# Feature columns in another order, sums over slots first, and another instruction list, in a fused attention and feed-forward kernel

## The chip, the cores and the metric

The kernel runs on one core of a Trainium2 chip. The metric is device time in microseconds (us) of one execution; before the change the median of three runs is 409.5 us (409.31 to 409.65). The engines are named as the profile names them: PE is TensorE (matmuls), PEld its weight loads, DVE is VectorE, ACT is ScalarE, POOL is GpSimd, SP is SyncE, which here issues nearly all transfers.

## What is computed

One transformer block on x of 2048 rows and 576 columns, in bf16. A vector c gives six modulation vectors (`silu(c) @ w_mod`): shift, scale and gate for each of two halves.

```
h = layernorm(x) * (1 + ca) + sa
x = x + ga * A(h)            # attention with feature maps, 32 heads of 18
h = layernorm(x) * (1 + cb) + sb
x = x + gb * (relu(h @ w1) @ w2)      # 576 -> 4608 -> 576
```

The attention has no score matrix. Queries and keys go through a map of 18 x 18 per head, and each gives 36 features:

```
q, k, v = split(h @ wqkv)                       # heads of 18
pq, pk = q @ w_phi[h], k @ w_phi[h]
phi = concat([softmax(p), softmax(-p)], -1)     # over the 18 features of a head
kv = phi_k^T v;  z = sum over rows of phi_k
o = (phi_q @ kv) / (phi_q @ z + 1e-6);  A = o @ wo
```

## The kernel before, in words

The 2048 rows are 16 tiles of 128 (four blocks of four tiles; eight units of two tiles). The work has three stages.

In the first, up to about 18 us, the weights are prepared. The key map is folded into the key weights: SP loads `kv_raw` (five chunks of the weights of keys and values, step `LK`) and the first blocks of x (`LP`); TensorE transposes each chunk (`fold_T`, step `WT`, line 341), DVE or ACT copies it out (`WTE`), TensorE multiplies by the maps (`fold`, `F1`, line 351), and DVE or ACT copies the result out in two pieces (`FA1`, `FB1`). Beside it run the layer norms of the first tiles (`LS` statistics, `RS` the reciprocal root, `LX` the normalization; the statistics of units 1, 4, 6 and 7 are on ACT, lines 230 and 231) and the modulation columns (`first_mods`, `MC1`, line 319, copied out at lines 324 to 328). `Z` is a dummy matmul (line 205).

In the second stage, 18 to 88 us, each tile's values, keys and queries are projected (`proj`, line 457; steps `V`, `K`, `Q`) into PSUM tiles of two banks, of which there are three (`mmp`), and copied out by ACT or DVE (`VE`, `KE`, `QE`, all at lines 88 and 90). The keys' features go through the softmaxes block by block. Then the products of features and values over all 16 tiles are summed (`kv_part`, `KVa` to `KVc`, line 636).

In the third, the eight units of queries are taken through their softmax, a transposing transfer (`q_T`, step `qT`, line 664, tile ET), the product with kv (`num`, line 677), the quotient, the product with wo, the second layer norm and the feed-forward (`ps_h` at line 807, ReLU at lines 863, 864 and 890, `ps_y` at line 907).

A tile's features stand in 11 groups of three heads. A group has 54 numbers per sign: 18 features by 3 heads, with the head innermost. Two features side by side make a slot of 6 numbers (pair, head), so there are 9 slots. The softmax of both signs is made by `softmax_parts`, for the keys on four tiles at a time (line 606), for the queries on two (line 616). The steps are, with the names in the order list (with a `q` in front for queries):

- `MN`, `MX` (`ext`): minimum and maximum over the features, a tree of operations on DVE (lines 474 to 479).
- `LO`, `HI` (`less`): minimum minus feature and feature minus maximum, written to the two halves of the group (lines 487 and 489), both into bf16.
- `EX`: exp on ACT, in place (line 516).
- `SU`, then `SA`: sums over the slots by TensorE, nine matmuls with the identity into PSUM (line 523), and over the pairs by DVE (line 527). Seven pairs of key tiles and one unit of queries go this way. All others take `SD` (`sums`, line 534): one reduction on DVE over all 18 features.
- `RC`: ln and exp on ACT, which make the reciprocal (lines 539 and 541); `SC`: scaling on DVE, one operation for keys (line 547) and one per sign for queries (line 551).

Within a group the layout is sign, slot, pair, head: 54 numbers of the one sign, then 54 of the other.

Instructions of SP, PE, DVE and ACT run in the order in which the code gives them. For the first 145 us or so that is the list of steps `order` in the kernel's text: a step is a name with its place (tile, chunk or unit), and a last number, where there is one more, says which of DVE and ACT takes a copy. After the list the blocks of the remaining units follow in loops (`block`), with fixed places for the softmax steps of the next units. A list item that stands earlier is ahead in the queue of each engine that it uses, transfers on SP included.

Of the kernel before, what the change touches and what calls it, by code (L numbers as in the profile page):

```python
# [43 lines left out]
def kernel(  # L44
# [419 lines left out]
    def softmax_parts(E, src, n, whole):  # L464
# [3 lines left out]
        def slots(a, s=0):  # L468
            return a[:, :, :, s * GF:(s + 1) * GF].rearrange("p n g (f c) -> p (n g) f c", c=G2)

        def ext(op):
            src_, w = src.rearrange("p n g c -> p (n g) c"), 4 * G2
            a = work.tile([P, 4 * NG, w], BF16, name="tree", tag="tree", bufs=1)[:, 0:ng]
            V.tensor_tensor(out=a, in0=src_[:, :, 0:w], in1=src_[:, :, w:2 * w], op=op)
            for w in (2 * G2, G2):
                V.tensor_tensor(out=a[:, :, 0:w], in0=a[:, :, 0:w], in1=a[:, :, w:2 * w], op=op)  # L476
            V.tensor_tensor(out=a[:, :, 0:G2], in0=a[:, :, 0:G2], in1=src_[:, :, 8 * G2:9 * G2], op=op)
# [40 lines left out]
        def sums_pe(j):  # L518

            ps = t["s", j] = aux_tile("ps_sum")[:, 0:2 * NG * 2 * G2].rearrange("p (a c) -> p a c", c=G2)  # L520
            e = E[:, j:j + 2].rearrange("p n g (s c) -> p (n g) s c", s=2)
            for f in range(DH // 2):
                T_.matmul(ps, lhsT=ident[:], rhs=e[:, :, :, f * G2:(f + 1) * G2], start=(f == 0), stop=(f == DH // 2 - 1))  # L523
# [6 lines left out]
        def sums(j):  # L530
            b, k = j // 2 * 2, j % 2
            if ("l", b) not in t:
                t["l", b] = work.tile([P, 4 * NG, GH], FP32, name="ln_s", tag="ln_s", bufs=2)
            V.tensor_reduce(out=t["l", b][:, k * 22:(k + 1) * 22].rearrange("p (g s) h -> p g s h", s=2), op=ALU.add,  # L534
                            axis=mybir.AxisListType.X, in_=E[:, j].rearrange("p g (s f h) -> p g s h f", s=2, h=GH))
# [7 lines left out]
        def scale(j):  # L543
            r = t["r", j][:].rearrange("p a e h -> p a (e h)")
            if whole:
                e = E[:, j:j + 2].rearrange("p n g (s f c) -> p (n g s) f c", s=2, c=G2)
                V.tensor_tensor(out=e, in0=e, in1=r.unsqueeze(2).to_broadcast([P, 4 * NG, DH // 2, G2]), op=ALU.mult)
                return
            for s in range(2):
                e, q = slots(E[:, j:j + 2], s), r.rearrange("p (a s) c -> p a s c", s=2)[:, :, s]  # L550
                V.tensor_tensor(out=e, in0=e, in1=q.unsqueeze(2).to_broadcast([P, 2 * NG, DH // 2, G2]), op=ALU.mult)
# [13 lines left out]
    def pad_keys(b):  # L565
        G.memset(phik_g(b)[:, :, NG - 1, 0:GF], 0.0)
# [17 lines left out]
    def features(dst, ps, eng):  # L584

        copy(eng, dst[:, 0:10, :].rearrange("p (a g) c -> p a g c", a=2),
             ps[:, :, 0:5 * GF].rearrange("p a (g c) -> p a g c", c=GF))
        copy(eng, dst[:, 10, :].rearrange("p (f h) -> p f h", h=GH)[:, :, 0:2],
             ps[:, 1, 5 * GF:5 * GF + 36].rearrange("p (f h) -> p f h", h=2))

    def keys_out(t, eng):
        features(phik_g(t // TPB)[:, t % TPB, :, 0:GF], pss["k", t], eng)

    def queries_out(t, eng):
# [4 lines left out]
        features(pq[b][:, j], pss["q", t], eng)  # L599
# [5 lines left out]
    def k_soft(b):  # L605
        return softmax_parts(phik_g(b), phik_g(b)[:, :, :, 0:GF], TPB, True)
# [3 lines left out]
    def q_soft(n):  # L610
# [5 lines left out]
        return softmax_parts(E[:, :, :, 0:DW], pq[b][:, u * U:(u + 1) * U], U, False)  # L616
# [356 lines left out]
    LH LK.0 Z.21 LP.1 SIL CR LP.0 Z.22 Z.11 LK.4 Z.3 WT.0 LS.3 LS.1 LK.1 LS.2 WT.4 Z.8 WBD WTE.4 WT.1 WTE.1.1 WTE.0  # L973
    LK.2 RS.1 Z.20 WT.2 LK.3 LS.0 LA F1.1 LX.1 RS.0 WTE.2.1 WT.3 FA1.1 FB1.1 WTE.3.1 LX.0 LP4.2 Z.23 F1.2 F1.4 FB1.4.1
    FB1.2.1 Z.24 FA1.4.1 PT.1 MC1.0 PX.1.0 PX.1.1 PT.0 PX.0.0.1 FA1.2 F1.0 FA1.0 PX.0.1 F1.3 MC1.1 MC1.2 FA1.3.1
    FB1.0.1 MSC MSH SCv.2 FB1.3.1 SCv.0 LP4.4 SCv.3 Bv SCv.4 LP4.6 SCv.1.1 BEv.0.1 LQ.1 B1 LS.6 OPEN BE1.1.1 LQ.5
    BEv.1.1 SC1.0 SC1.3 PM.0 LS.5 V.3 BE1.0.1 V.1 LQ.4 SC1.4.1 V.0 LQ.3 VE.3 LS.4 SC1.2 LS.8 SC1.1 VE.1 PM.2 VE.0 RS.2
    LQ.2 LS.7 LQ.0 LX.2 LS.12 V.2 K.0 K.1 LT.5 RS.3 VE.2.1 KE.0.1 LT.4 LS.9 KE.1.1 K.2 KE.2 F0.0 LS.11 K.3 FB0.0.1
    FA0.0.1 F0.4 LS.13 LX.3 PM.1 FA0.4 FB0.4 V.5 LS.10 KE.3 VE.5 RS.4 SC0.0 V.4 LT.7 VE.4 F0.2 FB0.2.1 FA0.2.1 MN.0
    LO.0 SC0.4.1 K.5 LT.6 F0.1 K.7 LX.4 KE.5 K.6 FA0.1.1 FB0.1 LO.1 F0.3 SC0.2 LM.2 MX.0 LT.8 SC0.1 KE.7 FA0.3.1 K.4  # L980
    FB0.3.1 KE.6 SC0.3 KE.4 MN.1 RS.5 B0 BE0.1.1 V.7 LX.5 LM.0 BE0.0.1 LS.14 LM.1 HI.1 PM.3 Q.2 LT.10 VE.7 QE.2 RS.6
    Q.1 HI.0 K.8 QE.1 LT.11 Q.7 KE.8.1 MX.1 EX.0 QE.7 LS.15 Q.0 LX.6 Q.3 LO.3 QE.0 RS.7 SU.0 K.10 LT.9 QE.3.1 HI.3 K.11
    K.9 EX.1 KE.11 LO.2 WOL qMN.0 SA.0 LX.7 KE.10 KE.9 LT.12 SU.1 HI.2 EX.3 K.12 RW.1 RW.0 MN.2 SA.1 qMX.0 KE.12 LT.15
    SU.3 RWE.0.1 LT.14 K.15 RC.0 W1 qLO.0 K.14 RWE.1.1 LO.4 EX.2 KE.15 qHI.0 LT.13 Q.14 LO.5 MX.2 SA.3 KE.14 qEX.0
    QE.14 K.13 V.9 RC.1 HI.5 SU.2 HI.4 RC2.0 KE.13 MN.3 Q.4 LW.1.1 LO.7 VE.9 qEX.1 SA.2 V.8 EX.4 EX.5 QE.4.1 Q.13 MX.3
    V.6 VE.8 LO.6 SC.0 qSU.0 V.13 RC.2 SC.2 VE.6 qSA.0 RD.2 QE.13 Q.12 SU.5 RC.3 HI.6 VE.13 SC.3 qRC.0 V.10 EX.6 SU.4
    VE.10 SA.5 RC2.2 V.11 RC.5 QE.12 VE.11 qSC.0 V.12 SA.4 HI.7 EX.7 SC.1 SD.12 Q.8 V.15 RD.0 SD.13 SC.5 VE.12 VE.15
    SU.7 RC.4 SA.7 SC.4 RC.6 V.14 qT.0 QE.8 KVa LW.1.0 SC.6 VE.14 RC.7 KVb RC2.1 SC.7 LW.0.0 KVc Q.11 WS.1 KVE.0 LW.2.1
    KVE.1 LW.0.1 QE.11 WS.0 NU.1 Q.6 NU.0 NUE.1 OT.1 Q.10 NUE.0 qMN.1 OT.0 OTE.1 QE.6 OTE.0 MCE2 WO.1 QE.10 WOE.1 WO.0
    WOE.0 S2.1.1 R2.1 S2.0 R2.0 Q.15 X2.1 X2.0 Q.9 qLO.1 PN.1 PN.0 QE.15 PNE Q.5 QE.5 QE.9 qMX.1 qHI.1 qEX.3 HA.0 HA.1  # L990
    HA.2 qMN.2 HB.0 LW.2.0 P2 HB.1 qSD.3 qEX.2 HB.2 qSD.2 LW.3.1 qMX.2 LW.3.0 W2.0.0 W2.1.0 RL.0 W2.0.1 HA.3 RL.1 qRC.1
    RL.2 RD.1 HA.4 HB.3 HB.4 HA.5 RL.3 HA.6 W2.2.1 HB.5 RL.5 qSC.1 HB.6 W2.1.1 qT.1 NV.0 RL.6 Y.1.0.0 NVE.0 W2.2.0 OU.0
    NV.1 qHI.2 RL.4 Y.1.0.1 HA.7 qLO.2 NVE.1 qEX.4 qSD.4 qEX.5 HA.8 OU.1 WA.0 HB.7 WB.0 qSD.5 WPE.0 qRC.2 HB.8 RL.7
# [131 lines left out]
```

## Time and profile before

| what | us |
|---|---|
| median of three runs | 409.5 (409.31 to 409.65) |
| the profiled execution | 409.36 |
| its span, first to last instruction | 407.6 |
| busy in the span: PE | 399.2 (98%) |
| DVE | 232.3 (57%) |
| ACT | 181.7 (45%) |

The profile comes from one execution. A row of operations gives line, engine, operation, output<-input with shapes, the count after x, then busy time and the mean ns of one; behind the second bar stands the idle time of the engine just before them and what ended it. A row of the wait view gives engine, operation and what it waited for: total us, times, longest. A row of the timeline begins with its start and its duration in us. A row of the chain (start, duration, engine, tile, line, count) follows back from the last instruction what released what. A row of the stage view gives the stretch and its length, then busy us and instructions of PE, PEld, DVE, ACT and POOL, the granted clock, the share of the DMA engines and GB/s. The mean ns of a matmul is its latency: matmuls overlap, so the time that one adds to a row of them is taken from the chain.

### The profile page before, as it was taken

To read this page: it belongs to the slowest core of one execution; us is meant where nothing else is said; L and a number is where in the kernel's file an instruction comes from. 1 tells how busy PE (TensorE), PEld (TensorE's weight loads), DVE (VectorE), ACT (ScalarE), POOL (GpSimd) and SP (SyncE) were. 2 spreads that over 40 slices of the span, in tenths; PEclk is the share of its full clock that TensorE was granted. 3 is DMA by queue.
4 is the path that set the end of the run, shared out by engine and by line. 5 is a ranking of instruction groups with operands and counts; after the bars stand their busy time and mean duration, and the time that the engine had idled before them with its cause. 6 is when DMAs were issued, how large, how long until landed. Compare 5 with 4: busy or idle time off the path is not lost.

```text
span 407.6 us, 10671 instructions
## 1 busy us (share of the span) xinstructions
PE 399.2 (98%) x4572; PEld 298.3 (73%) x4572; DVE 232.3 (57%) x603; ACT 181.7 (45%) x337; POOL 19.4 (5%) x123
## 2 busy tenths in 40 slices
PE   6899999999999999999999999999999999999997
PEld 3777777797877888888888888655467774447776
DVE  6889999999766756685886579423202310000111
ACT  5899999938653065216422450144530005552000
POOL 8100000000000000000000000000000000000000
PEclk9999999999999999999999999999999999999999
DMA  8968950499973401423374216400040000000001
GB/s 235 290 109 214 210 128 17 75 262 370 279 180 72 95 3 34 89 60 58 70 98 83 38 21 129 71 2 1 2 66 16 14 31 2 0 2 2 14 18 29
DMA packets 71001, 35.53 MB, mean 87 GB/s; under 512 B 56673, under 2 KB 67434, under 8 KB 70954
## 3 DMA queue, kind: packets, MB, share of 16 engines
q1 hardware_dynamic: 70352, 34.83, 37.9%
q8 instruction: 36, 0.59, 0.6%
q10 hardware_dynamic: 602, 0.02, 0.1%
q14 instruction: 11, 0.09, 0.1%
HBM read 19.27 MB, written 2.37 MB: 53 GB/s over the span
## 4 chain that ended last, share of the span: by engine, by line
PE 89%; DVE 5%; DMA 2%; ACT 1%; issue 1%; SPq 0%; ACTq 0%
PE ps_y L907 35%; PE ps_h L807 31%; PE ps_v L457 5%; PE ps_k L457 5%; PE ps_wo L807 4%; PE ps_q L457 3%; PE ps_sum L523 2%; DMA kv_raw<-in_A_wqkv_dram 1%; PE ps_kv L636 1%; DMA ET<-room 1%; PE ps_num L677 1%; DVE ln_s L534 1%; DVE tree L476 1%; PE ps_bias L372 1%; DVE xn L239 0%
## 5 line engine op out<-in xcount | busy, mean ns | idle before, releaser
L907 PE MATMUL ps_y<-w_sb,H 128*128 128x288 bf16 x864 | 109.3, 286 | 0.0
L907 PEld LDWEIGHTS <-H 128*128 128x128 bf16 x864 | 82.9, 98 | 22.3 <-issue 2.0
L807 PE MATMUL ps_h<-hT2all,w1a 64*128 64x256 bf16 (+1 forms) x960 | 78.5, 305 | 0.0
L915 DVE TENSOR_TENSOR outt<-ps_y,row_gb 128x288 bf16<-128x288 f32 (+2 forms) x33 | 14.7, 445 | 103.0 <-PE ps_y L907 103.0
L807 PEld LDWEIGHTS <-w1a 64*128 64x128 bf16 x960 | 46.8, 94 | 22.0
L807 PE MATMUL ps_h<-hT2all,w1b 64*128 64x256 bf16 (+1 forms) x768 | 62.8, 305 | 0.0
L863 ACT ACTIVATE H<-ps_h 128x512 bf16<-128x512 f32 x36 | 21.5, 596 | 81.3 <-PE ps_h L807 81.3
L457 PEld LDWEIGHTS <-hT 128*128 128x128 bf16 x480 | 46.1, 97 | 12.2 <-issue 0.4
L890 ACT ACTIVATE H<-ps_h 128x1024 bf16<-128x1024 f32 x36 | 36.0, 1018 | 37.8 <-PE ps_h L807 37.8
L807 PEld LDWEIGHTS <-w1b 64*128 64x128 bf16 x768 | 37.4, 94 | 18.0
L724 DVE TENSOR_TENSOR x_sb<-x_sb,ps_wo 128x288 bf16<-128x288 bf16 x28 | 11.4, 450 | 42.4 <-PE ps_wo L807 42.4
L807 PE MATMUL ps_h<-hT2all,w1c 64*128 64x256 bf16 (+1 forms) x216 | 33.4, 305 | 0.0
L907 PE MATMUL ps_y<-w_sb,H1m 128*128 128x288 bf16 (+2 forms) x270 | 32.4, 273 | 0.0
L907 PEld LDWEIGHTS <-H1m 128*128 128x128 bf16 x270 | 24.5, 98 | 5.2
L516 ACT ACTIVATE room<-room 128x1188 bf16<-128x1188 bf16 x16 | 18.6, 1189 | 15.7 <-DVE room L489 13.9
L811 POOL MEMSET token<- 1x2 bf16 x86 | 8.2, 96 | 311.8 <-PE ps_h L807 291.6
L457 PE MATMUL ps_q<-wfold,hT 128*128 128x270 bf16 (+1 forms) x160 | 21.6, 285 | 0.0
L457 PE MATMUL ps_v<-wv_sb,hT 128*128 128x288 bf16 x160 | 21.4, 286 | 0.1
L457 PE MATMUL ps_k<-wfold,hT 128*128 128x270 bf16 (+1 forms) x160 | 21.2, 285 | 0.0
L227 DVE BATCH_NORM_STATS2 bst<-x_sb 128x6 f32<-128x288 bf16 x46 | 18.6, 445 | 1.5 <-DMA x_sb<-in_A_x_dram 1.5
L534 DVE TENSOR_REDUCE ln_s<-room 128x66 f32<-128x1188 bf16 x14 | 18.7, 1368 | 0.0
L864 ACT ACTIVATE H1m<-ps_h 128x512 bf16<-128x512 f32 x30 | 17.8, 592 | 0.0
(156 smaller groups left out, 442.9 us busy)
## 6 DMA issues: line engine op xcount, KB each, us to landing
w_sb<-in_B_w_dram SPq DMA_DIRECT2D x6, 864.0 KB, 12.4
out_dram<-outt SPq DMA_DIRECT2D x15, 144.0 KB, 1.9
w1b<-in_B_w_dram SPq DMA_DIRECT2D x2, 1024.0 KB
x_sb<-in_A_x_dram SPq DMA_DIRECT2D x3, 576.0 KB, 10.3
w1a<-in_B_w_dram SPq DMA_DIRECT2D x2, 768.0 KB
kv_raw<-in_A_wqkv_dram SPq DMA_DIRECT2D x4, 288.0 KB, 5.0
wma<-in_w_mod_dram SPq DMA_DIRECT2D x2, 576.0 KB
wmb<-in_w_mod_dram SPq DMA_DIRECT2D x2, 576.0 KB
```

Source lines behind the costliest of these rows:

```text
L227: V.bn_stats(out=st[:, half, :], in_=x_sb[:, t0 + j, half * 288:(half + 1) * 288])
L457: T_.matmul(ps[:, 0:cn], lhsT=lhs[:, ci, :], rhs=w[:, ci, cs:cs + cn], start=(ci == 0), stop=(ci == KC - 1))
L516: A_.activation(out=E[:, j:j + k], in_=E[:, j:j + k], func=ACT.Exp)
L534: V.tensor_reduce(out=t["l", b][:, k * 22:(k + 1) * 22].rearrange("p (g s) h -> p g s h", s=2), op=ALU.add, axis=mybir.AxisListType.X, in_ ...
L724: V.tensor_tensor(out=xs[:, cs:cs + cn], in0=xs[:, cs:cs + cn], in1=p[:, 0:cn], op=ALU.add)
L807: i = T_.matmul(ps, lhsT=l, rhs=r, start=(phase == 0 and k < 2), stop=(phase == 1 and k >= len(items) - 2))
L811: g = last[key] = G.memset(token[:], 0.0)
L863: A_.activation(out=p2t["H1"].rearrange("p (e j) n -> p e j n", e=2)[:, :, i, :], in_=f1[i][:, :, 0:U * P], func=ACT.Relu)
L864: A_.activation(out=h1_more(i), in_=f1[i][:, :, U * P:], func=ACT.Relu)
L890: A_.activation(out=p2t["H1"].rearrange("p (e j) n -> p e j n", e=2)[:, :, 2 * q:2 * q + 2], in_=f1[q][:].rearrange("p e (h n) -> p e h n" ...
L907: T_.matmul(ps[:, 0, 0:cn], lhsT=h, rhs=p2t["w2"][:, k, c], start=(k == 0), stop=(k == NJ - 1))
L915: V.tensor_tensor(out=o[:, c], in0=ps[:, 0, 0:cn], in1=rows["gb"][:, c], op=ALU.mult)
```

## The change

The layout within a group becomes slot, sign, pair, head: 12 numbers per slot, 6 of each sign. With it:

- The copies of keys out of PSUM write runs of 6 into every second run (`features`, `keys_out`); queries keep their compact form until `less` spreads them.
- A sum matmul reads 12 numbers side by side per group instead of twice 6.
- `sums` is two operations: a reduction over the 9 slots into 132 fp32 numbers (tile `ln_e`) and an addition of the two pairs, 66 numbers.
- `scale` is one operation for queries too.
- The tile `root` has three buffers instead of four.
- The list has the same 476 steps in another order, and 23 of its copies or scalings change between DVE and ACT. Everything after the list stays.

```
-            e = E[:, j:j + 2].rearrange("p n g (s c) -> p (n g) s c", s=2)
+            e = signs(E[:, j:j + 2])
             for f in range(DH // 2):
-                T_.matmul(ps, lhsT=ident[:], rhs=e[:, :, :, f * G2:(f + 1) * G2], ...)
+                T_.matmul(ps.rearrange("p (a s) c -> p a (s c)", s=2), lhsT=ident[:], rhs=e[:, :, f], ...)
...
-            V.tensor_reduce(out=t["l", b][:, k * 22:(k + 1) * 22].rearrange("p (g s) h -> p g s h", s=2), op=ALU.add,
-                            axis=mybir.AxisListType.X, in_=E[:, j].rearrange("p g (s f h) -> p g s h f", s=2, h=GH))
+            s = work.tile([P, 2 * NG, G2], FP32, name="ln_e", tag="ln_e", bufs=1)
+            V.tensor_reduce(out=s.rearrange("p (g s) c -> p g (s c)", s=2), op=ALU.add, axis=mybir.AxisListType.X,
+                            in_=E[:, j].rearrange("p g (f c) -> p g c f", c=2 * G2))
+            V.tensor_tensor(out=t["l", b][:, k * 2 * NG:(k + 1) * 2 * NG], in0=s[:, :, 0:GH], in1=s[:, :, GH:], op=ALU.add)
...
-            for s in range(2):
-                e, q = slots(E[:, j:j + 2], s), r.rearrange("p (a s) c -> p a s c", s=2)[:, :, s]
-                V.tensor_tensor(out=e, in0=e, in1=q.unsqueeze(2).to_broadcast([P, 2 * NG, DH // 2, G2]), op=ALU.mult)
+            e, r = signs(E[:, j:j + 2]), t["r", j][:].rearrange("p (a s) e h -> p a (s e h)", s=2)
+            V.tensor_tensor(out=e, in0=e, in1=r.unsqueeze(2).to_broadcast([P, 2 * NG, DH // 2, 2 * G2]), op=ALU.mult)
...
-    LH LK.0 Z.21 LP.1 SIL CR LP.0 Z.22 Z.11 LK.4 Z.3 WT.0 LS.3 LS.1 LK.1 LS.2 WT.4 Z.8 WBD WTE.4 WT.1 WTE.1.1 WTE.0
+    LH LP.1 LK.1 SIL Z.20 Z.23 LK.0 WBD LK.2 LK.4 Z.22 LS.3 Z.8 LS.2 RS.1 WT.0 WT.2 LP.0 WT.1 WTE.0 Z.21 LK.3 WTE.2.1
```

The first place is the start of SP's queue; `kv_raw` are the weight chunks, `x_sb` the blocks of x, `wma` the first modulation weights. Before:

```order
L154 DMA kv_raw<-in_A_wqkv_dram 128x1152
L102 DMA x_sb<-in_A_x_dram 128x1152 x2
L154 DMA kv_raw<-in_A_wqkv_dram 64x1152
L154 DMA kv_raw<-in_A_wqkv_dram 128x1152 x3
L161 DMA wma<-in_w_mod_dram 64x1152
```

After, at the same place of SP's queue:

```order
L102 DMA x_sb<-in_A_x_dram 128x1152
L154 DMA kv_raw<-in_A_wqkv_dram 128x1152 x3
L154 DMA kv_raw<-in_A_wqkv_dram 64x1152
L102 DMA x_sb<-in_A_x_dram 128x1152
L154 DMA kv_raw<-in_A_wqkv_dram 128x1152
L161 DMA wma<-in_w_mod_dram 64x1152
```

An x block goes ahead of all weight chunks, the second x block moves behind four of them, and the first chunk that TensorE transposes (`WT.0`, chunk 0) is now third. The last chunk is seventh in both.

The second place is ACT at the first projections; `v` are copies of values out of PSUM, lines 230 and 231 statistics, `rstd` the reciprocal root. Before:

```order
L362 ACTIVATE wfold_88<-room,mod_402 64x576
L88 ACTIVATE v_93<-ps_v 128x32x18
L230 ACTIVATE room,mv<-x_sb 128x576
L231 ACTIVATE room,mv<-x_sb,mv 128x576
L88 ACTIVATE v_93<-ps_v 128x32x18 x2
L234 ACTIVATE rstd<-mv,eps_t 128x2
L235 ACTIVATE rstd<-rstd 128x2
```

After, ACT at the same place:

```order
L362 ACTIVATE wfold_88<-room,mod_402 128x576
L88 ACTIVATE v_93<-ps_v 128x32x18
L230 ACTIVATE room,mv<-x_sb 128x576
L231 ACTIVATE room,mv<-x_sb,mv 128x576
L234 ACTIVATE rstd<-mv,eps_t 128x2
L235 ACTIVATE rstd<-rstd 128x2
L88 ACTIVATE v_93<-ps_v 128x32x18 x2
```

The two instructions of the reciprocal root have moved ahead of the second and third copy of values.

The third place is DVE ahead of the first quotient of the second unit: `ln_s` (and `ln_e`) are the sums, `tree` and `root` the next unit's maximum, `room<-room,rsum` the scaling, after which the transfer to ET starts. Before:

```order
L534 TENSOR_REDUCE ln_s<-room 128x66 x2
L474 TENSOR_TENSOR tree<-room 128x528
L476 TENSOR_TENSOR tree<-tree 128x22x12
L476 TENSOR_TENSOR tree<-tree 128x22x6
L477 TENSOR_TENSOR tree<-tree,room 128x22x6
L479 TENSOR_TENSOR root<-tree 128x132
L551 TENSOR_TENSOR room<-room,rsum 128x22x54 x2
L685 TENSOR_SCALAR rq<-ps_num 128x24
```

After, DVE at the same place:

```order
L538 TENSOR_REDUCE ln_e<-room 128x132
L540 TENSOR_TENSOR ln_s<-ln_e 128x66
L538 TENSOR_REDUCE ln_e<-room 128x132
L540 TENSOR_TENSOR ln_s<-ln_e 128x66
L550 TENSOR_TENSOR room<-room,rsum 128x22x108
L477 TENSOR_TENSOR tree<-room 128x528
```

The five operations of the maximum now follow the scaling. On PE one more half of `ps_h` (step `HA.7`) stands ahead of the first `ps_num` of that unit (step `NV.0`).

91 lines of the change are left out of this document (44 added, 47 removed).

## Prediction

> **What bounds the kernel now.** I read the page's busy line first, then TensorE's waits, then the busy time by stage.
>
> ```profile
> PE 399.2 (98%) x4572; PEld 298.3 (73%) x4572; DVE 232.3 (57%) x603; ACT 181.7 (45%) x337; POOL 19.4 (5%) x123
> PE ps_wT L341 <- DMA kv_raw<-in_A_wqkv_dram: 1.7, 1, 1.7
> PE ps_warm L205 <- DVE ccol L168: 1.2, 1, 1.2
> PE ps_fold L351 <- ACT wT L88: 0.5, 1, 0.5
> PE ps_num L677 <- DMA ET<-room: 0.2, 1, 0.2
> 0.00:18.00 18.00, 13.13 (x166) 9.41 (x167) 13.36 (x46) 11.59 (x27) 8.83 (x28) 1.00 1.05 286
> 18.00:83.00 65.00, 64.93 (x578) 50.62 (x577) 61.80 (x138) 62.06 (x133) 2.34 (x11) 1.00 0.62 126
> 88.00:118.00 30.00, 29.61 (x422) 24.39 (x419) 23.22 (x64) 18.55 (x35) 0.62 (x7) 1.00 1.02 297
> 160.00:260.00 100.00, 100.00 (x1316) 82.35 (x1314) 76.36 (x209) 32.49 (x42) 2.42 (x24) 1.00 0.41 73
> ```
>
> TensorE (PE, third column of the stage rows) is busy 98% of the span, and its waits by the wait view are small and nearly all before 13 us. In the first 18 us it is busy 13.1; from there on it hardly stops. So a microsecond is won in three ways only: cheaper TensorE instructions, a shorter start, or one of the few later waits. In the second stage VectorE (61.8 of 65) and ScalarE (62.1 of 65) are almost as full: there a gain of TensorE lasts only as long as those two keep up.
>
> **The change part by part.**
>
> *The sums on TensorE.* 72 matmuls with an identity add up the slots (eight steps of nine). The chain gives what one takes when TensorE does nothing else:
>
> ```profile
> 46.25 1.19 PE ps_sum L523 x9
> 47.44 3.68 PE ps_k L457 x30
> L523 PE MATMUL ps_sum<-phik,ident 128*128 128x264 bf16 x63 | 9.5, 296 | 0.0
> L457 PE MATMUL ps_k<-wfold,hT 128*128 128x270 bf16 (+1 forms) x160 | 21.2, 285 | 0.0
> ```
>
> A projection matmul takes 3.68 / 30 = 123 ns for 288 columns on average (270 and 306 in turn), 0.426 ns a column. A sum matmul has 264 columns, which would be 112 ns, but takes 1.19 / 9 = 132 ns. The 20 ns more go with its right-hand side, which is read in 44 runs of 6 numbers where the projection reads one run: about 0.45 ns a run. After the change it is 22 runs of 12, so I estimate 122 ns. The ends are 132 (no gain) and 112 (a full one): 0 to -1.4 us for the 72, and taken is 72 x -10 to -11 ns = **-0.8 us**. All of it lies on TensorE, before the keys' products at 83 us.
>
> *The operations on VectorE.* These rows have one shape each.
>
> ```profile
> L534 DVE TENSOR_REDUCE ln_s<-room 128x66 f32<-128x1188 bf16 x14 | 18.7, 1368 | 0.0
> L551 DVE TENSOR_TENSOR room<-room,rsum 128x1188 bf16<-128x1188 bf16 x16 | 11.7, 772 | 0.3
> L547 DVE TENSOR_TENSOR phik<-phik,rsum 128x2376 bf16<-128x2376 bf16 x8 | 10.8, 1386 | 0.0
> L477 DVE TENSOR_TENSOR tree<-tree,phik 128x264 bf16<-128x264 bf16 x8 | 2.4, 297 | 0.3
> L476 DVE TENSOR_TENSOR tree<-tree 128x264 bf16<-128x264 bf16 x24 | 7.3, 305 | 0.8
> L685 DVE TENSOR_SCALAR rq<-ps_num 128x24 f32<-128x24 f32 x16 | 2.8, 178 | 7.8 <-PE ps_num L677 7.6
> L685 DVE TENSOR_SCALAR rq<-ps_nun 128x8 f32<-128x8 f32 x14 | 2.2, 155 | 0.0
> ```
>
> Scaling the queries becomes one operation of 2376 in place of two of 1188: 1386 against 2 x 772 = 1544, -0.16 us in each of eight units. Each of the 16 sums on VectorE gains an addition of 66 numbers: 155 to 178 by the two smallest rows plus 0.04 for the width, about +0.2 us. Together +2 us of VectorE, of which two sums (+0.4) and one scale (-0.16) lie before the keys' products. Reading a step's input in runs of 6 costs nothing: line 477 reads one such run in every 54 or 108 columns and takes 297, against 305 for line 476, which reads its own tile. So the minima, maxima and subtractions keep their times, and the copies out of PSUM write runs of 6 and are taken as unchanged.
>
> The sum itself is the unknown price. It now reads numbers 3 apart (1368 for 1188); afterwards 12 apart. Nothing in the trace reads bf16 so far apart; the nearest is line 685, with 19 fp32 numbers between reads: (178 - 155) / 16 = 1.44 ns a number, against (1368 - 155) / 1188 = 1.02 in the sum. So the ends are 0 and +0.42 x 1188 = +0.5 us a sum; nothing shows a reduction quicker than 1.02, so no gain. I take 0, since it is still one number at a time. [...]
>
> *The order of the start.* The first weight chunk is now the third transfer instead of the first, an x block the first. Landings in queue order are read from who waited:
>
> ```profile
> 4.86 0.85 PE L341 MATMUL ps_wT<-ident,kv_raw 128*108 128x128 bf16 x6
> 4.92 0.68 ACT L230 ACTIVATE room<-x_sb 128x576 bf16<-128x576 bf16 x1 [1.13 <-DMA x_sb<-in_A_x_dram]
> 6.67 0.82 DVE L227 BATCH_NORM_STATS2 bst<-x_sb 128x6 f32<-128x288 bf16 x2 [1.50 <-DMA x_sb<-in_A_x_dram]
> 7.37 0.88 PE L341 MATMUL ps_wT<-ident,kv_raw 128*108 128x128 bf16 x6 [1.66 <-DMA kv_raw<-in_A_wqkv_dram]
> 10.50 0.52 PE L341 MATMUL ps_wT<-ident,kv_raw 128*108 128x128 bf16 x6
> 15.85 0.42 DVE L90 COPY hT<-psT_h 128x512 bf16<-128x512 bf16 x1
> 16.33 0.14 DVE L328 CAST room<-ps_mod 64x1 bf16<-64x1 f32 x1
> 17.79 0.91 PE L457 MATMUL ps_v<-wv_sb,hT 128*128 128x288 bf16 x6
> ```
>
> The third transfer landed by 6.67, the fourth by 7.37. So the first transposes move from 4.86 to about 6.7. The last weight chunk is the seventh transfer in both orders and its transposes came at 10.50. Four groups of 0.85 fit between 6.7 and 10.5, so the last chunk still sets the pace: no loss here, and up to +1.8 if that is wrong (a rival). After it VectorE's work ahead of the modulation columns (line 328) shrinks by about 0.6 us, three copies of hT of 0.42 to 0.56 going to ScalarE and one back, against two fold copies of 0.3 and small exchanges. A dummy matmul stands behind it, so I count half: **-0.3 us** (0 to -0.6) at the first projection, 17.79 before.
>
> *ScalarE's order in the first projections.*
>
> ```profile
> 19.87 0.65 ACT L88 ACTIVATE v<-ps_v 128x576 bf16<-128x576 f32 x1
> 21.99 1.17 ACT L88 ACTIVATE v<-ps_v 128x576 bf16<-128x576 f32 x2
> 23.05 0.29 ACT L234 ACTIVATE rstd<-mv,eps_t 128x2 f32<-128x2 f32 x1
> 23.48 0.67 ACT L230 ACTIVATE room<-x_sb 128x576 bf16<-128x576 bf16 x1
> 22.70 3.84 PE L457 MATMUL ps_k<-wfold,hT 128*128 128x270 bf16 x30
> ```
>
> TensorE has three PSUM tiles. Its fifth projection (22.70) takes the tile that the second copy frees at about 22.6. In the new order the rstd pair (23.05 to 23.48, 0.43) stands ahead of that copy, which then ends at 23.05, while TensorE arrives 0.3 earlier, at 22.4 to 22.6. So it waits: **+0.5 us** (0 to 0.9). What is queued behind the rstd pair on ScalarE is just these copies, and TensorE waits for them.
>
> *Up to the keys' products.* Between the first projection and the keys' products two copies of keys or queries leave VectorE on balance; a row copy and a fold copy come to it, and the 0.2 of sums and scale.
>
> ```profile
> 82.85 5.23 PE L636 MATMUL ps_kv<-v,phik 128*128 128x57 bf16 x176
> 82.87 4.00 DVE L547 TENSOR_TENSOR phik<-phik,rsum 128x2376 bf16<-128x2376 bf16 x3
> L90 DVE CAST phik<-ps_k 128x540 bf16<-128x540 f32 (+1 forms) x6 | 2.4, 449 | 0.1
> ```
>
> A copy (two instructions) is 2.4 / 3 = 0.8 us there, so VectorE has -1.6 + 0.4 + 0.4 + 0.2 = -0.6 us; ScalarE, which takes what it gives and gives what it takes, has about 0.7 more. The last key scale ends at 86.87; the last 22 of 176 products need it at 82.85 + 5.23 x 154/176 = 87.4. The slack of 0.55 is kept: both move earlier by 0.6 to 0.9. Nothing is counted.
>
> *The first wait for a transposed query.* VectorE no longer takes the next unit's maximum (five operations) ahead of the scale, and TensorE gets one more half of ps_h (1.1 us) ahead of the products.
>
> ```profile
> 111.94 2.35 PE L807 MATMUL ps_h<-hT2all,w1b 64*128 64x256 bf16 x40
> 114.51 0.41 PE L677 MATMUL ps_num<-KVZ,ET 108*128 108x57 bf16 x8 [0.23 <-DMA ET<-room]
> 155.62 4.80 PE ps_h L807 x88
> ```
>
> One ps_h matmul takes 4.80 / 88 = 54.5 ns, so the 40 end at 114.1 and TensorE stands 0.4 us. With the transposed query earlier and its use later the wait goes: **-0.4 us**. The copies of wo's input are the next to be late, but two steps of ps_y lie ahead of them as before.
>
> Everything after 145 us is code in the old order, with TensorE at 100 of 100 and VectorE at 76: the added sums hide there.
>
> **Sum.** -0.8 - 0.3 + 0.5 - 0.4 = -1.0 us. The profiled execution took 409.36 (span 407.6 and 1.76 around it), so 408.36; the median of the runs is 0.14 above it, so **408.5 us**.
>
> **The rivals.**
> 1. *Everything pays* (0.13): the sum matmul reaches 112 ns (-1.4) and the copy at 22.6 is in time. -1.4 - 0.3 - 0.4 = -2.1: 407.4. For it: only the run length sets the matmul apart from the projection. Against: ScalarE is at 62 of 65 already.
> 2. *The slots-first sum is slow* (0.17): 0.5 us more for each of 16 sums, 8 us of VectorE. Before the products that is +1.0, which eats the slack and 0.1 to 0.3 of TensorE; the wait for the query comes back (0.4). 409.0 to 409.2, take 409.0. For it: the rate of line 685. Against: that row is a small operation in PSUM. [...]
> 3. *ScalarE takes over before the products* (0.15): its 0.7 us more makes the last reciprocals late, and what the sum matmuls gain is waited off again: -0.3 + 0.5 - 0.4 = -0.2, 409.3.
> 4. *The start is late* (0.13), slower: the first weight chunk as third transfer delays the chain of transposes, copies and folds as a whole, 4.86 to 6.67, +1.8. Then -0.8 + 1.8 + 0.5 - 0.4 = +1.1: 410.6. For it: TensorE waited for just these transfers (1.7). Against: the last chunk is no later. It makes the kernel slower from the point where the first projection starts 1.5 us later than 17.79.
>
> **How the numbers follow.** My forecast has 0.42. About 0.2% (0.8 us) is what a measurement of this kernel can tell from no change, so faster means below 408.7. Of the forecast three quarters lie there (0.31), with all of rival 1 (0.13) and a little of rival 2 (0.03): 0.47. Slower is rival 4 with 0.02 of rival 3: 0.15. The rest, 0.38, is the same. The range goes from rival 1 (407.4) over rivals 2 and 3 to 410.0; it leaves out most of rival 4 and a little below.
>
> **What would show it.** Right: nine sum matmuls in about 1.1 us on the chain; sums of about 1.37 with additions of 0.2 behind; the first projection at 17.2 to 17.8; a short wait for a value copy near 22.5; no wait at the first ps_num of the second unit. Wrong: sums near 1.9 (rival 2), a gap in front of the last key products with ScalarE as releaser (rival 3), a first projection after 18.6 (rival 4), or a sum matmul still at 132.

## The result and the profile after

The changed kernel takes 416.41 us (median of six runs, 416.19 to 417.43) against 409.4 us for the kernel before it on the same chip (408.96 to 409.67): a ratio of 1.0177, 95% interval 1.0163 to 1.019. It is slower by 7 us, where the prediction had it faster by 1.

The busy line of the changed kernel's page, to be read beside that of before:

```profile
PE 401.0 (97%) x4571; PEld 299.8 (72%) x4572; DVE 250.1 (60%) x605; ACT 184.3 (44%) x346; POOL 20.2 (5%) x123
```

From TensorE's wait view of the changed kernel (total us, times, longest; waits in the first 18 us are mostly left out):

```profile
PE ps_num L676 <- DVE o_tm L688: 1.9, 3, 1.1
PE ps_wT L341 <- DMA kv_raw<-in_A_wqkv_dram: 1.2, 2, 1.0
PE ps_kv L635 <- DVE phik L550: 1.2, 2, 0.7
PE ps_wo L806 <- DMA oT<-o_tm: 0.8, 1, 0.8
PE ps_h L806 <- ACT H L889: 0.8, 1, 0.8
PE ps_h L806 <- POOL token L810: 0.8, 3, 0.3
```

And from its stage view (length; busy us and instructions of PE, PEld, DVE, ACT and POOL; clock, DMA share, GB/s):

```profile
18.00:83.00 65.00, 64.08 (x591) 50.37 (x590) 61.80 (x131) 60.93 (x130) 2.80 (x9) 1.00 0.67 147
88.00:118.00 30.00, 27.84 (x400) 22.57 (x402) 25.16 (x58) 18.15 (x39) 0.62 (x7) 1.00 0.72 231
160.00:260.00 100.00, 99.13 (x1333) 83.90 (x1329) 83.78 (x199) 35.35 (x48) 2.42 (x26) 1.00 0.40 64
```

TensorE's own work is about as long as before (401.0 against 399.2 us); what is new are waits, spread over the whole kernel, and most of their releasers are VectorE's or stand behind VectorE (`o_tm` is the quotient, `phik` the scaled keys). VectorE has 17.8 us more to do. The groups of operations that the prediction priced show where that comes from (mean ns of one after the busy time):

```profile
L538 DVE TENSOR_REDUCE ln_e<-room 128x132 f32<-128x1188 bf16 x14 | 31.8, 2273 | 1.8 <-ACT room L519 1.5
L540 DVE TENSOR_TENSOR ln_s<-ln_e 128x66 f32<-128x66 f32 x16 | 3.7, 229 | 0.5
L550 DVE TENSOR_TENSOR room<-room,rsum 128x2376 bf16<-128x2376 bf16 x8 | 11.1, 1388 | 1.1 <-ACT rsum L546 0.8
L490 DVE TENSOR_TENSOR phik<-root,phik 128x1188 bf16<-128x1188 bf16 x8 | 6.1, 776 | 0.1
L88 ACT ACTIVATE phik<-ps_k 128x540 bf16<-128x540 f32 x13 | 8.1, 627 | 0.0
```

The reduction over the slots takes 2273 ns where the one over all features took 1368: +0.9 us in each of 16, 14.5 us of VectorE. The rest came as priced: the addition of pairs 229 ns, the scale 1388 ns. The subtractions with runs of 6 (776 against 771 ns) and the copies of keys that write them (627 against 616 ns) cost next to nothing.

The table gives TensorE's timeline at six places (start, in us, of the first projection, of the first product of keys, end of the last one, start of the first `ps_h` and of the 51st `ps_y` matmul, end of the last matmul), for before, after, and the experiments that follow.

| kernel | first projection | keys' products | their end | first ps_h | 51st ps_y | end |
|---|---|---|---|---|---|---|
| before | 17.79 | 82.85 | 88.08 | 100.35 | 128.11 | 404.52 |
| after | 17.19 | 82.32 | 89.16 | 101.81 | 132.48 | 411.52 |
| dense reads | 17.19 | 81.70 | 87.35 | 100.00 | 129.56 | 406.21 |
| dense reads in the blocks only | 17.19 | 82.31 | 89.16 | 101.81 | 132.54 | 409.18 |
| new list only | 17.49 | 83.27 | 88.50 | 101.16 | 130.85 | 407.33 |
| new list, old columns, mended stage | 17.68 | 83.46 | 88.70 | 101.34 | 129.31 | 405.79 |
| pairs first | 17.18 | 81.71 | 86.94 | 99.59 | 129.05 | 405.58 |
| pairs first, list of before | 17.61 | 82.22 | 88.16 | 100.44 | 128.91 | 405.43 |
| second mixed list | 17.19 | 81.72 | 86.95 | 99.61 | 128.06 | 404.54 |

From before to after TensorE wins 0.6 us at the start, and then loses: 1.6 us in the keys' products (6.84 us long instead of 5.23), 0.4 up to the first `ps_h`, 2.9 in the first feed-forward block (30.67 instead of 27.76), 2.6 in the blocks behind it, and 0.1 before the products. That is the 7.0 us.

### The profile page after: what moved, and what is told of

Its sections match the earlier page's. It is cut to its first block, busy times and chain, and to the rows that moved or that the text cites. A ratio compares the mean times of both kernels' runs of the same rounds, so it can differ in the third digit from the quotient of the medians.

```text
span 414.4 us, 10672 instructions
## 1 busy us (share of the span) xinstructions
PE 401.0 (97%) x4571; PEld 299.8 (72%) x4572; DVE 250.1 (60%) x605; ACT 184.3 (44%) x346; POOL 20.2 (5%) x123
## 4 chain that ended last, share of the span: by engine, by line
PE 64%; DVE 26%; DMA 4%; ACT 3%; issue 2%; POOL 0%; DVEq 0%; POOLq 0%
PE ps_h L806 28%; PE ps_y L906 26%; DVE ln_e L538 5%; PE ps_wo L806 3%; DVE phik L550 2%; DVE tree L479 2%; PE ps_k L457 2%; DMA x_sb<-in_A_x_dram 2%; DVE xn L239 2%; DVE bst L227 1%; DVE tree L477 1%; DVE phik L492 1%; ACT room L519 1%; DMA oT<-o_tm 1%; DVE phik L490 1%
## 5 line engine op out<-in xcount | busy, mean ns | idle before, releaser
L538 DVE TENSOR_REDUCE ln_e<-room 128x132 f32<-128x1188 bf16 x14 | 31.8, 2273 | 1.8 <-ACT room L519 1.5
L544 ACT ACTIVATE ln_s<-ln_s 128x132 f32<-128x132 f32 x16 | 5.1, 316 | 39.1 <-DVE ln_s L540 36.7
```

The lines of the kernel that those rows point to most:

```text
L538: V.tensor_reduce(out=s.rearrange("p (g s) c -> p g (s c)", s=2), op=ALU.add, axis=mybir.AxisListType.X, in_=E[:, j].rearrange("p g (f c) ...
```

## The experiments

### The sum, the list and the columns apart

The theory after the result was S: numbers 24 bytes apart make the sum slow, and TensorE waits for what hangs on it. The rivals were R (short results make it slow, nine numbers each instead of eighteen) and O (the new list makes the waits).

Dense reads: the changed kernel, with one edit in the sum. The nine numbers of a result then lie side by side; they are other numbers than the softmax needs.

```
-                            in_=E[:, j].rearrange("p g (f c) -> p g c f", c=2 * G2))
+                            in_=E[:, j].rearrange("p g (c f) -> p g c f", c=2 * G2))
```

> The changed kernel, but the sum on VectorE reads nine numbers that lie side by side instead of nine that lie 12 apart; the sums are therefore of other numbers than the softmax needs, everything else (132 results, the addition behind it, the order) stands. Theory S (the numbers 24 bytes apart make the sum slow, and VectorE's 16 x 0.9 us are what TensorE waits for): sums at 1.4 us or less, VectorE 14 us less busy, no wait for the last key scales near 86 and 88 us, total 408 to 409.5. Theory R (it is the 132 short results of nine numbers instead of 66 of eighteen): the sum stays at 2.27 us and the total at 416.4. Theory O (the new order makes the waits, whatever the sum takes): the sum is quick, but the total stays at 414 to 416.

411.0 us, ratio to before 1.0044 (1.0027 to 1.006). The group of its sums:

```profile
L538 DVE TENSOR_REDUCE ln_e<-room 128x132 f32<-128x1188 bf16 x14 | 19.2, 1373 | 1.9 <-ACT room L519 1.5
```

With as many results of nine numbers each the sum takes 1373 ns, so R falls. The slow sum is worth 5.4 us of the 7. But 1.4 us more than before are left by the medians (1.8 by the ratio), and S had said 408 to 409.5. So something else in the change costs too; the next runs look for it in the list.

The new columns with the list of before (`order` of the one text in the other):

> The new columns and sums with the list in the order of before. Theory S: the two sums of every unit still cost VectorE 2 x 1.1 us more, TensorE waits for the same results, less the 1.2 us that the 72 sum matmuls win: 411 to 415. Theory O: 408 to 409, the matmuls' gain alone. Theory R gives the same as S here.

419.11 us, ratio 1.024 (1.0219 to 1.026): more than any theory had. Under the slow sum the new list is quicker than the old by 2.6 to 2.7 us (ratios, medians); without it, as later runs show, it isn't. By estimate about 1.7 us of that are a lower clock: in this run's profile TensorE waits 1.78 us for the key scales, and from 87 to 91 us, right behind that wait, the granted clock is 0.56 to 0.58 (4 us x 0.43; by the stage view 0.93 in the mean of 83 to 88 us and 0.96 of 88 to 118, and 0.996 over the whole execution). By that estimate about 1 us is left for the order of the list itself.

The old columns with the new list:

> The old columns and sums with the list in the new order. Theory S and R: no slow sum, so 408.5 to 410 (the earlier first projection wins 0.6 us, small waits for value copies give about as much back). Theory O: 414 to 416, with the waits for key scales near 86 and 88 us and for the transposed queries as in the changed kernel.

412.5 us, ratio 1.0072 (1.0056 to 1.0088). Neither theory: the list alone costs 3 us. By the table 1.9 of it lie between the first `ps_h` and the 51st `ps_y`.

### What the distance costs

The changed kernel with this at the second last feed-forward block:

```
+            flat = room[:, 3 * TPB * DP:3 * TPB * DP + 1188]
+            for c, f in ((1, 9), (3, 9), (4, 9), (6, 9), (8, 9), (12, 9), (16, 9), (22, 9), (3, 18), (6, 18), (1, 18)):
...
+                for i in range(3):
+                    V.tensor_reduce(out=s[:, 0:a * c].rearrange("p (a c) -> p a c", c=c), op=ALU.add, axis=mybir.AxisListType.X,
+                                    in_=flat[:, 0:a * c * f].rearrange("p (a f c) -> p a c f", f=f, c=c))
```

> The changed kernel with 33 more sums on VectorE at the second last feed-forward block, where it is idle most of the time: each reads about 1188 numbers, with 1, 3, 4, 6, 8, 12, 16, 22 or 24 bf16 numbers between two that are added, in results of nine or of eighteen numbers; nothing uses the results. Theory S: about 1.37 us up to some distance between 3 and 12, and 2.2 to 2.3 us at 12 and more, the same for nine and for eighteen. Theory R: 2.2 us wherever nine are added, 1.37 where eighteen are, at any distance. [...]

Its total, 431.98 us, holds the added work and isn't compared. The groups of the added sums. The number in the name is the distance between two numbers that are added (s12x: 12 numbers, 24 bytes); 128 or 132 results are sums of nine numbers, 66 of eighteen.

```profile
L1092 DVE TENSOR_REDUCE s12x<-room 128x132 f32<-128x1188 bf16 x3 | 6.8, 2275 | 0.1
L1092 DVE TENSOR_REDUCE s8x<-room 128x128 f32<-128x1152 bf16 x3 | 6.7, 2248 | 0.1
L1092 DVE TENSOR_REDUCE s16x<-room 128x128 f32<-128x1152 bf16 x3 | 6.7, 2240 | 0.1
L1092 DVE TENSOR_REDUCE s22x<-room 128x132 f32<-128x1188 bf16 x3 | 6.7, 2233 | 0.1
L1092 DVE TENSOR_REDUCE s6x<-room 128x132 f32<-128x1188 bf16 x3 | 5.4, 1807 | 0.1
L1092 DVE TENSOR_REDUCE s6x<-room 128x66 f32<-128x1188 bf16 x3 | 5.2, 1720 | 0.1
L1092 DVE TENSOR_REDUCE s3x<-room 128x66 f32<-128x1188 bf16 x3 | 4.2, 1391 | 0.1
L1092 DVE TENSOR_REDUCE s3x<-room 128x132 f32<-128x1188 bf16 x3 | 4.2, 1391 | 0.1
L1092 DVE TENSOR_REDUCE s4x<-room 128x132 f32<-128x1188 bf16 x3 | 4.2, 1391 | 0.1
L1092 DVE TENSOR_REDUCE s1x<-room 128x132 f32<-128x1188 bf16 x3 | 4.2, 1388 | 0.1
```

The price has three steps: 1.39 us at 2, 6 and 8 bytes, 1.72 to 1.81 at 12, and 2.23 to 2.28 at 16, 24, 32 and 44 bytes. At 6 bytes it is the same for sums of nine and of eighteen (1391 ns). The kernel before read at 6 bytes, on the flat part; the change went to 24, past the last step. What the runs show are the steps; no run shows what makes them.

### Whether VectorE's idle time hides the sums of the later blocks

Dense reads in the ten sums of the last five units only:

```
-        return lambda: getattr(q_open(m), name)(*a)
+        return lambda: getattr(q_open(m), name)(*a, *([True] if name == "sums" else []))
```

(`sums` takes the flag and chooses the dense reads by it.)

> The changed kernel with dense reads only in the ten sums of the last five units, which lie in the blocks after 145 us; they add other numbers than the softmax needs. Theory S by stages (TensorE loses 2.4 us to the slow sums behind 145 us by the two traces, since each sum stands in a chain that ends in a transposed query): 413.7 to 414.3. Rival (the prediction's reason, that VectorE with 76 of 100 busy hides them there, and the loss comes down from the stages before): 416.0 to 416.5.

413.83 us, ratio 1.0109 (1.0095 to 1.0123), in the range of S by stages. The slow sums cost 2.6 us where VectorE has 84 of 100 us busy. How they do it is seen in the changed kernel's timelines, here of VectorE and TensorE in the third block (start, duration; idle time before in brackets):

```profile
248.45 2.28 DVE L538 TENSOR_REDUCE ln_e<-room 128x132 f32<-128x1188 bf16 x1
251.02 2.28 DVE L538 TENSOR_REDUCE ln_e<-room 128x132 f32<-128x1188 bf16 x1
254.16 0.61 DVE L688 TENSOR_TENSOR o_tm<-ps_num,rq 128x432 bf16<-128x432 f32 x1
255.81 1.39 DVE L550 TENSOR_TENSOR room<-room,rsum 128x2376 bf16<-128x2376 bf16 x1
```

```profile
246.51 0.40 PE L676 MATMUL ps_num<-KVZ,ET 108*128 108x57 bf16 x8
254.91 0.39 PE L676 MATMUL ps_num<-KVZ,ET 108*128 108x57 bf16 x8 [0.57 <-DVE o_tm L688]
264.16 0.39 PE L676 MATMUL ps_num<-KVZ,ET 108*128 108x57 bf16 x8 [1.10 <-DVE o_tm L688]
```

The products of 246.51 are ready at once, but their quotient stands behind both sums in VectorE's queue until 253.5, and the products at 254.91 wait for it. The one at 264.16 waits for the next quotient. VectorE has idle time in this block, but not where TensorE waits.

The same at the keys' products, where the scales stand behind two sums:

```profile
82.32 2.68 PE L635 MATMUL ps_kv<-v,phik 128*128 128x57 bf16 x88
85.74 2.12 PE L635 MATMUL ps_kv<-v,phik 128*128 128x57 bf16 x66 [0.75 <-DVE phik L550]
88.36 0.80 PE L635 MATMUL ps_kv<-v,phik 128*128 128x57 bf16 x22 [0.49 <-DVE phik L550]
```

### A true sum that is quick

Pairs first, slots second: the same two operations exchanged, so that the reduction is half as long and reads 12 bytes apart.

```
+            s = work.tile([P, 4 * NG, 4 * G2], BF16, name="tree", tag="tree", bufs=1).rearrange("p a c -> p (a c)")
+            s = s[:, 0:NG * DW // 2].rearrange("p (g f c) -> p g f c", f=DH // 2, c=G2)
+            e = E[:, j].rearrange("p g (m c) -> p g m c", c=G2)
+            V.tensor_tensor(out=s.rearrange("p g f (s h) -> p g (f s) h", h=GH), in0=e[:, :, :, 0:GH], in1=e[:, :, :, GH:], op=ALU.add)
+            V.tensor_reduce(out=t["l", b][:, ...].rearrange("p (g s) h -> p g (s h)", s=2), op=ALU.add,
+                            axis=mybir.AxisListType.X, in_=s.rearrange("p g f c -> p g c f"))
```

> The changed kernel with the two halves of its sum exchanged: first the two numbers of a pair are added (594 results, runs of three numbers), then nine numbers that lie 6 apart (12 bytes) are summed. From the probe (1807 ns for 1188 at that distance) and the additions of the page the two take 0.98 + 0.47 = 1.45 us, against 2.28 + 0.23 = 2.51 in the changed kernel and 1.38 + 0.23 = 1.61 with the dense reads. Theory S (only VectorE's time in the sum counts): 410.4 to 411.2, a little under the run with dense reads. If the dense reads were quick for a reason that a true sum doesn't share: 413 or more.

410.54 us, ratio 1.0031 (1.002 to 1.0043), within the expected range; the two operations take 0.56 and 0.99 us:

```profile
L541 DVE TENSOR_REDUCE ln_s<-tree 128x66 f32<-128x594 bf16 x16 | 15.8, 986 | 0.5
L540 DVE TENSOR_TENSOR tree<-room 128x594 bf16<-128x594 bf16 x14 | 7.8, 555 | 1.8 <-ACT room L519 1.5
```

With the list of before:

> The new columns with the list of before, and the pairs added first as in the run beside it. Theory S with the order as a second cost of its own (T: about 2 us of the new list lie in the first feed-forward block): 408.0 to 409.2, the 1.2 us of the sum matmuls under the kernel before, less what the 16 sums still cost more. If the columns themselves cost something besides the sum (copies, three root buffers instead of four): 410 or more.

410.05 us, ratio 1.0023 (1.0014 to 1.0033): over the expected range, and where the rival had it (410 or more). In both, nine sum matmuls on TensorE take 1.04 us in the chain where the old columns have 1.19, so the matmuls win 8 x 0.15 = 1.2 us. A row of the chain with the new list:

```profile
50.10 1.04 PE ps_sum L526 x9
```

The table shows where that goes with the list of before: the first product of keys is 0.6 us earlier, the last one 0.1 us later, since TensorE waits 0.5 us for the last scale (by its wait view), and 0.8 us more for transposed queries. With this list, what TensorE wins in front of VectorE's results it stands waiting for them. With the new list the gain stays: from the first projection to the keys' products the pairs-first kernel takes 64.53 us and the old columns 65.78, 1.25 us more, and neither waits inside the products.

### What the list costs in the first feed-forward block

The first idea was T. The two halves of the rows of `ps_h` (steps `HA`, `HB`) are held in order by a token that GpSimd writes. In the new list three second halves follow right behind their own first half, and TensorE waits 0.21 to 0.27 us each time (0.8 in the wait view). Moved apart:

```
-... HA.0 P2 LW.2.0 QE.9 LW.3.1 HB.0 QE.6 HA.1 RL.0 ... HA.5 RL.3 HB.5 W2.1.0 qHI.2 HA.6 HB.6 qT.1 RL.5 HA.7 RL.6 HB.4 NV.0
+... HA.0 P2 LW.2.0 QE.9 LW.3.1 QE.6 HA.1 HB.0 RL.0 ... HA.5 RL.3 HB.4 HB.5 W2.1.0 qHI.2 HA.6 qT.1 RL.5 HA.7 HB.6 RL.6 NV.0
```

> The changed kernel with three second halves of the rows of ps_h (HB.0, HB.5 and HB.6) moved in the list so that another half stands between each and its own first half, as in the list of before; HB.4 comes earlier for it. Theory T (a second half that directly follows its first waits for GpSimd's token, 0.21 to 0.27 us each): three waits fewer, 0.7 us less, 415.7. Rival: TensorE waits right behind for ScalarE's ReLU and for wo's input anyway (0.8 us each), so 0 to 0.2 us: 416.2 to 416.4.

> Both of the edits above in the new list: pairs first, and the three second halves moved. Theory T: 0.7 us less than with the pairs first alone, 409.8 to 410.4. Rival (the wait for wo's input, 0.6 us, grows by what the tokens give): the same as with the pairs first alone.

The first takes 417.4 us, ratio 1.0205 (1.0191 to 1.0219), 1 us more than the changed kernel; the second 410.42, ratio 1.0027 (1.0017 to 1.0038), the same as pairs first alone. The token waits are gone in both, and nothing is won: T falls. TensorE's timeline in the first of them:

```profile
115.19 0.29 PE L806 MATMUL ps_h<-hT2all,w1c 64*128 64x256 bf16 x2 [1.24 <-ACT H L889]
120.02 0.40 PE L676 MATMUL ps_num<-KVZ,ET 108*128 108x57 bf16 x8 [1.60 <-DMA ET<-room]
```

The first lies above both ranges that were expected of it, the second where the rival had it. Why the first got slower led to the next theory. The first ReLU (`RL.0`) now ends 0.7 us later, the exponentials of the second unit stand behind it on ScalarE, and sums, scale and transposed query are all 0.7 us later in their turn. So theory V: in this block the end is set by the second unit's softmax, down to its transposed query (ET) and what is made from it, and the new list makes that chain longer. The timelines of VectorE in the kernel before and in the pairs-first kernel show it.

```profile
104.25 2.68 DVE L534 TENSOR_REDUCE ln_s<-room 128x66 f32<-128x1188 bf16 x2
106.85 0.42 DVE L474 TENSOR_TENSOR tree<-room 128x528 bf16<-128x528 bf16 x1
108.34 1.46 DVE L551 TENSOR_TENSOR room<-room,rsum 128x1188 bf16<-128x1188 bf16 x2
```

```profile
105.43 0.57 DVE L540 TENSOR_TENSOR tree<-room 128x594 bf16<-128x594 bf16 x1 [1.53 <-ACT room L519]
109.50 1.40 DVE L552 TENSOR_TENSOR room<-room,rsum 128x2376 bf16<-128x2376 bf16 x1 [0.83 <-ACT rsum L548]
```

Before, VectorE goes from the sums to the next unit's maximum and to the scale without a pause. In the new list it stands 1.5 us in front of the sums, since ScalarE does the ReLU ahead of the exponentials, and 0.8 us in front of the scale, since the maximum no longer fills the time of the reciprocal (that second pause delays nothing, as the last run shows). The scale starts 1.2 us later, though `ps_h` starts 0.8 us earlier.

Mixed lists test it: the new list, with the softmax of that unit placed as in the list of before, in the pairs-first kernel.

```
-QE.6 HA.1 RL.0 HA.2 qEX.2 qMN.2 W2.0.0 HA.3 qEX.3 HB.1 W2.0.1 RL.1 HB.2 RL.2 qSD.3 qSD.2 qRC.1 W2.2.1 qSC.1 HB.3 qMX.2 ...
+HA.1 QE.6 HA.2 qEX.3 HB.0 qEX.2 qMN.2 W2.0.0 HB.1 qSD.3 HB.2 RL.0 qSD.2 W2.0.1 RL.1 HA.3 qRC.1 RL.2 qMX.2 W2.2.1 qSC.1 ...
```

> Pairs first in the new columns and the new list, but the second unit's softmax placed as in the list of before between HA.0 and NV.0: its exponentials ahead of the first ReLU on ScalarE, the maximum of the next unit ahead of the scale on VectorE, and each second half of the rows with another half in front of it. Theory V (in the first feed-forward block TensorE waits for the transposed query, so the chain of VectorE and ScalarE there sets the time, and the new list makes that chain later): the first ps_num of that unit 1 to 1.5 us earlier than with the pairs first alone (116.1), total 409.0 to 409.6. Rival (the next wait, for wo's input near 122 us, takes it back): 410.2 to 410.6.

415.62 us, ratio 1.0142 (1.0118 to 1.0166): a miss, and for another reason than the rival's. The edit had also moved two loads of w2 behind the transposes of ET on SyncE's queue, and the wait view has

```profile
PE ps_y L908 <- DMA w_sb<-in_B_w_dram: 3.1, 1, 3.1
```

Behind this wait, from 122 to 126 us, the granted clock was 0.53 and then 0.62, another 1.7 us by the same estimate (2 x 0.47 + 2 x 0.38), and 0.996 in the mean of this execution; the one execution of five with a mean clock of 0.999 took 413.4.

With the loads ahead of the transposes again, and `HA.7` behind `NV.1` in the one and ahead of `NV.0` in the other:

> The same idea as the run before it, with two things of that run undone: the two w2 loads stand ahead of the transposes of the second unit's queries on SyncE's queue again, and HA.7 stands behind NV.1 as in the list of before. Theory V (the chain to the transposed query sets the time of the first feed-forward block): no wait for w2 (3.1 us) and none of 1 us for the ReLU, the first ps_num of that unit at 114.5 to 115.5, total 409.0 to 409.8. Rival (what the stage gains in front is waited off at the next place): 410.2 to 410.8.

> The same, but HA.7 stays ahead of NV.0 as in the new list, with all w2 loads of the first 18 chunks ahead of the transposes. Theory V: 409.2 to 410.0, the half HA.7 covering what is left of the wait for the transposed query. Rival, as beside it: 410.2 to 410.8; if HA.7 waits for a free ps_h buffer as in the run before, 411.

409.69 us, ratio 1.0018 (1.0009 to 1.0027), and 409.67, ratio 1.0014 (1.0005 to 1.0023). Against pairs first that is 0.9 us less by the medians and 0.5 to 0.7 by the ratios, whose intervals overlap; the trace is clearer, with the end 1.0 us earlier (404.54 against 405.58) and the first `ps_num` of the unit at 114.25 instead of 115.82. Part of that comes from TensorE's own order, since both lists also keep the halves of the rows apart. The run with pairs first and the halves apart, which has the softmax in the place of the new list, is therefore the closer comparison: 410.42, so the softmax's place is worth 0.7 us by the medians and 0.4 to 0.5 by the ratios. There SyncE starts to issue the transposes of ET at 111.64; in the third mixed list, with `HA.7` ahead of `NV.0` in both, at 110.50. V stands, with that size. TensorE's timeline of the second mixed list:

```profile
114.25 0.41 PE L678 MATMUL ps_num<-KVZ,ET 108*128 108x57 bf16 x8 [0.51 <-DMA ET<-room]
```

The old columns with this stage mended:

> The columns and sums of before with the second of the mixed lists. With the new list alone these columns took 412.5, of which the trace puts 1.9 us between the first ps_h and the 51st ps_y. Theory V (that loss is the later chain to the transposed query, whatever the columns): 1.0 to 1.5 us less than with the new list alone, 411.0 to 411.5. Rival (the loss there comes from the old columns' longer sums of matmuls in front of it, so the place doesn't matter): 412.3 to 412.7.

410.76 us, ratio 1.004 (1.0027 to 1.0053): 1.7 us under the new list alone by the medians, 1.3 us by the ratios. V had said 1.0 to 1.5. By the table the block is back at 27.97 us from 29.69. The loss in that stage belongs to the list and not to the columns. Of the list's 3 us about 1.6 remain; the profiled executions show 1.3 of them, by the table 0.6 before the keys' products, 0.4 up to the first `ps_h`, 0.2 in the first block and 0.1 behind it. The trace has a candidate for the first two. Before the products TensorE stands about 0.4 us each in front of two projections, near 23 and 26 us, for a value copy and a key copy, as in the changed kernel. Behind them the first `ps_num` takes 0.86 us instead of 0.47, while five small operations that write `KVZ` run on ScalarE until 90.39; before, VectorE had written all of it by 89.03. No run changed these places alone, so this cause is not shown.

The last run puts the maximum behind the scale again:

> As the second of the mixed lists, with the next unit's maximum behind the scale again (as the new list has it), since the trace of that run has the reciprocals ready at about 108.2 us and the scale starting at 108.9 behind the maximum. Theory V: scale, transpose and the first ps_num of the second unit 0.5 us earlier, no wait for the transposed query, total 409.0 to 409.4, level with the kernel before or 0.1% under it. Rival (wo's input is late in its place, as in the third mixed list): 409.6 to 409.8, no change against that run.

409.52 us, ratio 1.0009 (1.0 to 1.0018), level with the kernel before, and between the two figures that were expected; it does no better than the second and third mixed lists beyond the uncertainty. Its scale starts 0.7 us earlier (108.17 against 108.87 in the second list), so the maximum behind the scale does bring the scale forward:

```profile
108.87 1.39 DVE L552 TENSOR_TENSOR room<-room,rsum 128x2376 bf16<-128x2376 bf16 x1
```

```profile
108.17 1.40 DVE L552 TENSOR_TENSOR room<-room,rsum 128x2376 bf16<-128x2376 bf16 x1 [0.83 <-ACT rsum L548]
```

But the two issues of the transposes take SyncE 4.39 us instead of 3.16, and the product starts at 114.18, where the second list had it at 114.25:

```profile
110.33 3.16 SPq L665 DMA_TRANSPOSE ET<-room  x2
```

```profile
109.63 4.39 SPq L665 DMA_TRANSPOSE ET<-room  x2
```

Why the issue took longer stays open; the same pair took 3.95 us in the kernel before and 3.15 in the changed one. An earlier scale alone is thus not enough for an earlier product. No version beat the kernel before.

## Why the prediction was wrong, step by step

- **The price of the sum** was the step that failed. The prediction said that 0 is taken "since it is still one number at a time", with +0.5 us as the upper end. It is +0.9 us, beyond that end. The upper end came from line 685, a small operation that reads fp32 in PSUM, and it did not bound a read of bf16 in SBUF: there the distance decides, 1.39 us at 2, 6 and 8 bytes and 2.23 to 2.28 at 16 to 44, and the trace had no such row on the far side of the step. Rival 2 (0.17) had the slow sum, but took its price from the same row, +0.5 us where +0.9 was measured. No rival came near 416.4.
- **The cover** failed next. "TensorE at 100 of 100 and VectorE at 76: the added sums hide there" compared busy shares. With dense reads in the blocks alone 2.6 us come back. By the table the slow sum takes 0.6 us before the products, 1.2 in them, 1.1 in the first block and 2.4 behind it, 5.3 in all, where rival 2 had 0.5 to 0.7 and nothing behind 145 us.
- **The first wait for a transposed query.** The prediction counted -0.4 and argued that the scale comes sooner once the maximum is moved behind it, and that a half of `ps_h` more covers the rest. The first half of that is right: in the last run the scale does start 0.7 us sooner with the maximum behind it. What failed is that the move of the first ReLU ahead of the exponentials on ScalarE was given no term: VectorE stands 1.5 us in front of the sums for it, and the scale comes 1.2 us later, not sooner. With the quick dense sum this block is 1.8 us longer than before instead of shorter. The mixed lists showed the order of this stage to be worth 0.5 to 1.0 us with the new columns, the halves of the rows included, and 1.3 to 1.7 with the old.
- **The sum matmuls** came out better than taken: nine in 1.04 us instead of 1.19 (read in the pairs-first kernels, whose matmuls are the same), so -1.2 us instead of -0.8, within its ends. By the estimate of 0.45 ns a run it would have been 122 ns a matmul; 116 were measured. But in the changed kernel TensorE waits 1.2 us inside the keys' products for scales that stand behind the slow sums, so "The slack of 0.55 is kept" did not hold there; with pairs first and the new list it did.
- **The start** won 0.6 us, the good end of its range. Whether for the reason given wasn't tested; with the new list and the old columns it was 0.3 and 0.1 us. Rival 4, the late first weight chunk, did not come.
- **ScalarE's order in the first projections**: the wait for the value copy came at 22.49, and TensorE lost about 0.4 us (0.5 was taken). A second one, for a key copy on VectorE, had no step:

```profile
22.49 1.39 PE L457 MATMUL ps_v<-wv_sb,hT 128*128 128x288 bf16 x10 [0.23 <-ACT v L88]
25.50 2.62 PE L457 MATMUL ps_k<-wfold,hT 128*128 128x270 bf16 x20 [0.40 <-DVE phik L90]
```

- **Up to the keys' products**: the first product came 0.5 us earlier, where the steps in front of it summed to 0.6. That nearness is luck: the slow sum took 0.6 us there and the key copy 0.4, neither in the sum, and the matmuls and the start won 0.7 more than was taken.
- **Scale, addition, copies, subtractions** came as priced.

## What to carry to other kernels

Before a layout is changed for the sake of one reader, write down for every other reader how many bytes lie between two numbers that it takes one after the other, and price the one whose distance grows by a row at that distance; if there is none, the range has to hold far more than the nearest row says (here +0.5 us by that row, +0.9 measured). An engine's idle share did not say here what a longer operation on it costs (2.6 us behind 145 us, with VectorE busy for 84 of 100): follow what stands behind that operation in its queue and who waits for it. And a list of steps tuned to one price of an operation is worth something else at another: here the new list was 2.7 us quicker than the old with the slow sum (by estimate some 1.7 of them by the clock), was nearly level with it with the pairs added first (410.5 against 410.1), and lost 3 us to it with the old columns.

## What the runs showed of the hardware

A reduction of about 1188 bf16 numbers on VectorE takes 1.37 to 1.39 us where numbers that are added lie 2, 6 or 8 bytes apart, 1.72 to 1.81 at 12 bytes and 2.23 to 2.28 at 16, 24, 32 and 44 bytes, without a further rise among these four; at 6 bytes results of nine and of eighteen numbers both took 1391 ns. An addition of two bf16 numbers each, 594 results with runs of three numbers, took 0.56 us. A sum matmul of 264 columns read in 22 runs of 12 adds 1.04 / 9 = 116 ns, against 1.19 / 9 = 132 in 44 runs of 6. Twice a TensorE wait (1.78 and 3.13 us) was followed by about 4 us with a granted clock of 0.53 to 0.62; behind one of 1.60 us in the first run with the halves apart it stayed at 1.00 (118 to 160 us). Issuing the same two transposes took SyncE 3.15 to 4.39 us from one kernel to the next, and what sets that is open.
